# Superblock 1's second product by seven products of halves, sums of w_out made earlier, and 32 writes issued by GpSimd

## The chip, the cores and the metric

The kernel runs on one core of a Trainium2 chip. The metric is the device time of one execution in microseconds. Five engines take part: TensorE (PE, matrix products), VectorE (DVE), ScalarE (ACT), GpSimd (POOL) and SyncE (SP), which in this kernel issues DMA transfers. Each engine works through its own instructions in the order of the program and waits where an instruction needs what another engine or a transfer has not yet delivered.

## The reference

Attention inside chunks of 64 positions, then a feed-forward network on the result, whose rows are x [4608 tokens, 512]:

```python
scores = scale * np.matmul(q_c, k_c.transpose(0, 1, 2, 4, 3))     # q, k, v: [8, 8, 576, 64], chunk = 64
scores = scores - np.max(scores, axis=-1, keepdims=True)
attn = np.exp(scores)
attn = attn / (np.sum(attn, axis=-1, keepdims=True) + 1e-09)
out = np.matmul(attn, v_c)
...
x = np.ascontiguousarray(attn_out.transpose(0, 2, 1, 3)).reshape(B * S, H * D)
...
h = x @ w_in                                                      # [4608, 512] x [512, 2048]
g = np.where(h > 0.0, h, alpha * (np.exp(np.minimum(h, 0.0)) - 1.0))
return (g @ w_out).astype(np.float32)                             # [4608, 2048] x [2048, 512]
```

## The kernel before

**Tiling.** The tokens are taken in nine blocks of TB = 512, the 2048 hidden units in NF = 16 hidden tiles of 128. x @ w_in is called the first product here, g @ w_out the second. Every operand is split in a high and a low float32r part, and a product of two operands is three matmuls of 512 columns: high by high, high by low, low by high (`three`, L434, so nearly all big matmuls have that line). ACT copies the high part (`ghi`), POOL or DVE subtracts it to get the low one (`glo`). In a second product of hidden tile f and token tile tt the order on PE is hi·hi, lo·hi, hi·glo or the like.

**Stages.** Blocks 0 to 2 are plain: 192 + 192 big matmuls each. Blocks 0 and 1 also prepare the weights; block 2, called the third block below, is written out in `THIRD_BLOCK`, `EVEN` and `ODD`. The six other blocks form three superblocks of two. A superblock takes its first product by seven products of halves (Strassen's scheme in Winograd's form, 336 big matmuls for 384); the sums and differences of operand halves that this needs are made ahead and lie in DRAM: those of w_in in `a_dram`, those of w_out in `w_dram`. Superblocks 0 and 1 are written out by hand: eight pairs of hidden tiles (`FIRST_PAIR`, `SECOND_PAIR`, `PAIR`), and then a list of 16 lines, `KEPT`, in which the second product of the superblock's second block runs (`split_kept`, "G": ACT and POOL or DVE split one hidden tile). Their second product is direct: 384 big matmuls each, with w_out's low parts loaded again and again from `lo_dram` by `load_lo`. Superblock 2 is emitted by `Plan`, a list scheduler that holds jobs with a due time, a cost per engine, and the places read and written; its second product goes by seven products of halves too, with B operands from `w_dram` loaded into a ring of places.

**Attention.** One token tile of 128 tokens at a time, an item of the lists for each step. DVE transposes q and k (L351), takes maxima and sums and scales, and transposes the scores (L388); four transfers of 32 KB (`turned<-unturned`) swap parts of them.

**Sums of w_out.** Class `Sums` makes them for one j (two hidden tiles): `whole` a and b (high plus low), `sum` c and d (four subtractions of 128 x 256), `high` e (an ACT copy of 128 x 1024), `low` f (a subtraction of 128 x 1024), then the writes to `w_dram`. Eight of them are needed before superblock 2: j = 2 in superblock 0, 3, 0, 1 and 4 in superblock 1, j = 5, 6, 7 at the start of the plan. The four unsummed quarters of w_out go to `w_dram` as well: high parts by `write_raw` (12 transfers of 256 KB), low parts by `write_raw_low`, all from SP and in the second half of superblock 1.

**What sets the order.** Outside the plan every item is issued where the lists name it, on each engine in that order; SP's transfers also run in that order, and an instruction that waits holds up all behind it on its engine. The last lines set `dynamic_dma_scratch_size=512`.

Of the kernel before, what the change touches and what calls it, by code (L numbers as in the profile page):

```python
# [20 lines left out]
def kernel(  # L21
# [19 lines left out]
    nc = tc.nc  # L41
# [522 lines left out]
    class Sums:  # L564
# [34 lines left out]
        def write(self, which=(0, 1)):  # L599
            for lo in which:  # L600
# [5 lines left out]

    def sum_step(j: int, part: str):
        if part == "a":
            place = kept_st[j][:, :4 * TB] if j < 2 else flat(g_kept[:, {2: 8, 3: 8, 4: 0}[j]:][:, :4])
            early_sums[j] = Sums(j, place, [weights[0][3][:, (2 * j + i) % (NF // 2), :] for i in range(2)])  # L610
        sums = early_sums[j]
        if part in "ab":
            sums.whole("ab".index(part), nc.gpsimd if j in (2, 3) else nc.vector)
        elif part in "cd":
            for t in ((1, 3), (2, 4))["cd".index(part)]:
                sums.sum(t, nc.gpsimd if j in (2, 3) else nc.vector)
        elif part == "e":
            sums.high()
        elif part == "f":
            sums.low()  # L620
            sums.write((0,))
        else:
            sums.write((1,))

    def write_raw(n: int, lo: int):
        half, i = divmod(n, 3)
        row, col = W_PARTS[i + 1]
        for d in range(2):
            nc.sync.dma_start(
                out=w_dram[4 + i, 2 * half + d, :, :, lo, :],  # L630
                in_=weights[half][2 + lo][:, 4 * d + row:4 * d + 4:2, col * HALF:(col + 1) * HALF].bitcast(F32))

# [96 lines left out]
    class Pair:  # L729
# [22 lines left out]
        def product(self, i: int):  # L752
            to = y_ps if i in (2, 5, 3) else x_ps
            (ah, al), (bh, bl) = a_operand(i), b_operand(PRODUCTS[i][1])
            for k in range(2):
                three(to, ah[:, k, :], al[:, k, :], bh[:, k, :], bl[:, k, :],
                      i in (1, 2, 5) and k == 0, k == 1, onto=i not in (1, 2, 5))
            if self.g + 1 < 2 * NG:
                load_a(self.g + 1, i)

        def keep(self, i: int):
# [233 lines left out]
    def warm(n: int):  # L995
# [3 lines left out]
        for i in range(n):  # L999
# [76 lines left out]
    )  # L1076
    VECTOR = (0, 8, 9, 10, 11, 12, 13, 15)
    MORE_PAIR = {(1, "p1"): "a", (1, "p6"): "b", (1, "p7"): "c", (1, "p3"): "d", (2, "p5"): "e", (2, "p3"): "f",
                 (3, "p3"): "g"}
    FIRST_SUMS = {(7, "p2"): "w0a", (7, "p6"): "w0b", (7, "p5"): "w0c", (7, "p7"): "w0d", (7, "p4"): "w1a",  # L1080
                  (7, "p3"): "w1b"}
    MORE_KEPT = ({
        7: "w4a", 8: "w4b", 9: "w4c", 10: "w4d", 11: "w4e", 12: "w4f w4g",
    }, {
        0: "L0", 1: "L1", 2: "L2 w0e", 3: "L3 w0f", 4: "w0g", 5: "w1c", 6: "w1d", 7: "w1e W0",
        8: "w1f w1g W1", 9: "L4 L5 W2", 11: "R0 L6 W3", 12: "R1", 13: "L7 W4", 14: "R2", 15: "R3 W5",
    })
# [132 lines left out]
    for f in range(NF):  # L1220
# [69 lines left out]
    def do(item: str):  # L1290
# [6 lines left out]
        elif item[0] == "L":  # L1297
            write_raw_low(int(item[1]))
        elif item == "P":
            second_products()  # L1300
        elif item == "Q":
            second_next()
        elif item == "S":
            store(*unstored.pop())
        elif item[0] == "x" and len(item) > 1:
            name, cols = item[1:3], slice(TB)
            if item[1] == "B":
                name = item[1:4]
            elif item[3:4] in ("a", "b"):
                cols = slice(T2) if item[3] == "a" else slice(T2, TB)  # L1310
            prepare(name, cols)
        elif item[0] == "A":
            load_a(0, int(item[1]))
        elif item[0] == "R":
            load_entry(2 * ENTRIES + int(item[1]))
# [4 lines left out]
    run = (PLAIN - 1) * TB, o_tiles(), b_half_place  # L1320
    for f in range(NF):
        for item in THIRD_BLOCK.get(f, ODD if f % 2 else EVEN).split():
# [42 lines left out]

    x_ps, y_ps = [ps_h.tile([P, TB], F32, name="h") for _ in range(2)]
    preparing, pair = True, None
    for sb in range(2):
        n0 = (PLAIN + 2 * sb) * TB
        run = n0, o_tiles(), a_half_place  # L1370
        for g in range(NG):
            before, pair = pair, Pair(sb * NG + g)
            for item in ((FIRST_PAIR, SECOND_PAIR)[g] if not sb and g < 2 else PAIR).split():
                if item[0] == "p":
                    pair.product(int(item[1]))
                elif item[0] == "c":
                    pair.keep(int(item[1]))
                elif item[0] == "d":
                    pair.add(int(item[1]))
                elif item in "45":  # L1380
                    if before:
                        next(before.parts["3" if item == "5" else item], None)
                elif item in "123":
                    next(pair.parts[item])
                else:
                    do(item)
                for part in MORE_PAIR.get((g, item), "").split():
                    do(f"w{2 + sb}{part}")
                if sb and (g, item) in FIRST_SUMS:
                    do(FIRST_SUMS[g, item])  # L1390
        halves_kept, o_last = iter(range(NF)), o_tiles()
        run = n0 + TB, o_last, b_half_place
        for f, line in enumerate(KEPT):
            for item in line.split() + MORE_KEPT[sb].get(f, "").split():
                if item == "4":
                    next(pair.parts["4"], None)
                elif item == "G":
                    split_kept(next(halves_kept))
                else:
                    do(item)  # L1400

    LATE_SUMS = 5, 6, 7
    units = {}
    NSPLIT = 7
    STEP = 6 * 227
# [408 lines left out]
                for m, name in enumerate(("t1", "T1", "t3", "t2", "T2", "t4", "T4", "T3", "B22")):  # L1814
                    add_prepare(at + .5 * m, name, cols)

    T0 = 4 * 7 * PAIRS * 2
    leftover, queue[:] = list(queue), []
    for when, (job, f, tt, hi, lo) in zip([T0 - 1 + .05 * i for i in range(4)] + [T0 - .5 + .05 * i for i in range(4)],
                                        leftover):  # L1820
# [9 lines left out]
        if last:  # L1830
# [12 lines left out]
    def add_sums(t: float, j: int, turn: int):  # L1843
        made = {}

        def begin():
            made[0] = Sums(j, kept_st[turn][:, :4 * TB],
                           [weights[0][3][:, (2 * j + i) % (NF // 2), :] for i in range(2)])

        def load():  # L1850
            begin()
# [2 lines left out]
        def whole(engine):  # L1854
# [54 lines left out]
```

## Time and profile before

| | us |
|---|---|
| runs | 836.88, 841.43, 843.36 |
| median | 841.43 |
| profiled execution | 835.11 |
| its span, 15864 instructions | 833.3 |
| stretch 317 to 448: pairs of superblock 0 | 131 |
| stretch 448 to 492: KEPT of superblock 0 | 44 |
| stretch 492 to 672: superblock 1 | 180 |
| stretch 672 to 833: superblock 2 with the tail | 161 |

Durations below come from the one profiled execution, which was faster than the three timed runs. In the profile's rows a name stands for a tile, `out<-in`, a number such as L723 for a line of the kernel; SPq is SP's issue of transfers, and its duration includes what it waits for. The L numbers of before and after differ for one operation: the subtraction of a high part is L723 before and L744 after in the superblocks, L479 in the plain blocks in both.

### The profile page before, as it was taken

The page shows a single profiled execution, that of the slowest core. Times are in us where ns is not written, and L with a number is a line of the kernel's source. Part 1 is how long each engine was busy: PE and PEld are TensorE (multiplying, and loading weights), DVE is VectorE, ACT ScalarE, POOL GpSimd, SP SyncE. Part 2 cuts the span into 40 slices and gives each one's busy share as a digit, 9 for nine tenths or more (in the row PEclk, how much of TensorE's full clock was granted, in tenths as well). Part 3 has the DMA queues.
Part 4 walks back from the last instruction along what each step waited for, and adds up shares of the span by engine and source line. Part 5 has one row for each costly group of instructions (what it writes and reads, how often), then busy time and mean ns, then how long its engine had stood idle before and what let it go on. Part 6 is the DMA issues. An engine that isn't in the chain of part 4 may idle for free.

```text
span 833.3 us, 15864 instructions
## 1 busy us (share of the span) xinstructions
PE 815.4 (98%) x5901; PEld 666.6 (80%) x5901; DVE 587.8 (71%) x859; ACT 497.7 (60%) x853; POOL 152.7 (18%) x133
## 2 busy tenths in 40 slices
PE   7899999999999999999999999999999999999997
PEld 6788888878888888888888888877878887888885
DVE  5999997666775769665666866655667586557974
ACT  5999875444554447666656346655566356776551
POOL 0000014446311211411113213211115020000100
PEclk9999999999999999999999999999999999999999
DMA  9875855856687777698987677789838999665655
GB/s 256 251 219 199 262 168 160 273 184 205 228 227 225 206 200 216 191 262 243 269 261 232 188 198 209 201 238 243 260 98 253 310 324 287 194 187 199 220 187 148
DMA packets 204973, 185.09 MB, mean 222 GB/s; under 512 B 76896, under 2 KB 186976, under 8 KB 204896
## 3 DMA queue, kind: packets, MB, share of 16 engines
q1 hardware_dynamic: 204896, 184.08, 74.7%
q8 instruction: 47, 0.77, 0.4%
q14 instruction: 30, 0.25, 0.1%
HBM read 137.36 MB, written 42.99 MB: 216 GB/s over the span
## 4 chain that ended last, share of the span: by engine, by line
PE 90%; DMA 4%; ACT 2%; SPq 2%; DVE 1%; issue 1%; DVEq 0%; ACTq 0%
PE o L434 46%; PE h L434 38%; PE ps_a L248 2%; PE ps_a L256 2%; SPq L206 1%; DMA turned<-unturned 1%; DMA ring<-a_dram 1%; PE h L451 1%; DMA v_sb<-in_v_dram 1%; DMA st<-in_moe_w_in_dram 1%; DMA ring<-w_dram 1%; PE ps_a L315 1%; PE ps_a L270 0%; ACT e L712 0%; ACT xhi L425 0%
## 5 line engine op out<-in xcount | busy, mean ns | idle before, releaser
L434 PE MATMUL o<-wo_hi,ghi 128*128 128x512 f32 x352 | 138.9, 395 | 0.0
L434 PE MATMUL o<-wo_hi,glo 128*128 128x512 f32 x352 | 137.4, 390 | 0.0
L434 PE MATMUL o<-wo_lo,ghi 128*128 128x512 f32 x352 | 137.2, 390 | 0.0
L434 PE MATMUL h<-xhi,wi_hi 128*128 128x512 f32 x276 | 96.0, 395 | 0.7 <-ACT kept L762 0.7
L434 PE MATMUL h<-xlo,wi_hi 128*128 128x512 f32 x276 | 94.5, 389 | 0.0
L723 POOL TENSOR_TENSOR glo<-e,ghi 128x512 fp32r<-128x512 f32 x32 | 41.7, 1304 | 214.2 <-ACT ghi L721 214.2
L434 PEld LDWEIGHTS o<-wo_hi,glo 128*128 128x128 f32 x352 | 66.1, 188 | 14.6 <-DVE glo L479 0.9
L434 PEld LDWEIGHTS o<-wo_hi,ghi 128*128 128x128 f32 x352 | 66.1, 188 | 14.5 <-ACT ghi L476 0.2
L434 PEld LDWEIGHTS o<-wo_lo,ghi 128*128 128x128 f32 x352 | 66.1, 188 | 13.3
L434 PE MATMUL h<-xhi,wi_lo 128*128 128x512 f32 x180 | 70.2, 390 | 0.0
L434 PEld LDWEIGHTS h<-xhi,wi_hi 128*128 128x128 f32 x276 | 51.7, 188 | 12.2 <-ACT kept L762 1.1
L434 PEld LDWEIGHTS h<-xlo,wi_hi 128*128 128x128 f32 x276 | 51.8, 188 | 10.4
L434 PE MATMUL o<-wo_hi,wo_lo 128*128 128x512 f32 x192 | 59.8, 390 | 0.0
L471 DVE SCALAR_TENSOR_TENSOR e<-e,h 128x512 f32<-128x512 f32 x48 | 32.8, 684 | 25.6 <-ACT e L469 25.4
L434 PE MATMUL h<-wi_lo,wi_hi 128*128 128x512 f32 x192 | 50.7, 399 | 0.0
L510 POOL TENSOR_TENSOR kept<-wi_hi,wi_lo 128x512 f32<-128x512 f32 x16 | 21.3, 1349 | 156.6 <-DMA kept<-in_k_dram 115.6
L393 ACT COPY unturned<-turned 128x512 f32<-128x512 f32 x28 | 17.4, 621 | 52.2 <-DVE turned L388 51.4
L434 PE MATMUL h<-wo_lo,wi_hi 128*128 128x512 f32 x192 | 48.6, 389 | 0.0
L762 ACT COPY kept<-h 128x512 f32<-128x512 f32 x48 | 28.1, 586 | 32.9 <-PE h L434 32.7
L361 DVE TENSOR_REDUCE mx<-ps_a 128x8 f32<-128x512 f32 x28 | 19.3, 689 | 37.5 <-ACT xf L420 36.8
L716 DVE SCALAR_TENSOR_TENSOR g_kept<-e,g_kept 128x512 f32<-128x512 f32 x32 | 22.6, 705 | 32.6 <-ACT e L713 32.6
L468 ACT ACTIVATE e<-h 128x512 f32<-128x512 f32 x48 | 28.8, 599 | 27.3 <-PE h L434 24.9
(203 smaller groups left out, 1793.2 us busy)
## 6 DMA issues: line engine op xcount, KB each, us to landing
wi_hi<-a_dram SPq DMA_DIRECT2D x112, 256.0 KB, 4.9
wo_lo<-lo_dram SPq DMA_DIRECT2D x36, 512.0 KB, 5.8
ring<-a_dram SPq DMA_DIRECT2D x56, 256.0 KB, 3.6
ring<-w_dram SPq DMA_DIRECT2D x28, 512.0 KB, 3.7
kept<-in_q_dram SPq DMA_DIRECT2D x100, 128.0 KB, 3.5
kept<-in_k_dram SPq DMA_DIRECT2D x100, 128.0 KB, 4.0
v_sb<-in_v_dram SPq DMA_DIRECT2D x32, 256.0 KB, 5.7
st<-in_moe_w_in_dram SPq DMA_DIRECT2D x16, 512.0 KB, 4.5
```

Source lines behind the costliest of these rows:

```text
L206: nc.sync.dma_start(out=dst[p0:p0 + n], in_=src[b, :, s0:s0 + n, :].rearrange("h s d -> s h d"))
L248: nc.tensor.matmul(scores[halves[c], j, hp, :], lhsT=qT[halves[j], hp, halves[c]], rhs=kT[halves[j], hp, halves[c]], start=True, stop=True,)
L256: nc.tensor.matmul(x_ps[halves[j], c, hp, :], lhsT=v_sb[halves[c], 2 * hp + j, :], rhs=aT[halves[c], :, j * NK + hp], start=True, stop=True,)
L361: nc.vector.tensor_reduce(out=mx, in_=self.scores, axis=AX.X, op=ALU.max)
L393: nc.scalar.copy(out=unturned, in_=turned)
L434: nc.tensor.matmul(ps, lhsT=a, rhs=b, start=start, stop=stop, skip_group_check=onto)
L468: nc.scalar.activation(out=e, in_=h, func=AF.Relu, scale=-1.0)
L471: nc.vector.scalar_tensor_tensor(out=e, in0=e, scalar=-1.0, in1=h, op0=ALU.add, op1=ALU.max)
L510: nc.gpsimd.tensor_tensor(out=out, in0=a, in1=b, op=op)
L716: nc.vector.scalar_tensor_tensor(out=to, in0=e, scalar=-1.0, in1=c, op0=ALU.add, op1=ALU.max)
L723: engine.tensor_tensor(out=lo, in0=e, in1=hi.bitcast(F32), op=ALU.subtract)
L762: nc.scalar.copy(out=c21 if i == 4 else self.kept[i - 1], in_=x_ps)
```

## The change

Superblock 1 is no longer written out: the hand-written pairs and KEPT run once, for superblock 0, and `superblock(1)` and `tokens(1)` (eight attention tiles) go through the plan ahead of superblock 2. Its second product is by seven products of halves. Since `w_dram` is needed one superblock earlier, the sums of w_out move forward: j = 4, 5 into the third block, j = 0, 3 into the pairs, j = 1 into KEPT, j = 2, 6, 7 into the plan. Up to the plan they run on POOL, but for j = 1 on DVE, and their writes are cut in halves of 256 KB and issued by POOL. The 12 writes of unsummed high parts ("W0" to "W5", two each) are issued by POOL in KEPT; the low parts are written by SP in the second block. `load_lo` runs for 20 pairs of hidden tiles instead of 36 (5·NG, 3·NG), and there are 28 loads of `w_dram` more. In KEPT the splits given to DVE are now those of f = 0, 3, 4, 5, 15; three G items move within their line.

```diff
+        def write_half(self, lo: int, half: int, queue=nc.gpsimd):
+            of = slice(2 * half, 2 * half + 2)
+            queue.dma_start(
+                out=w_dram[of, self.j // 2, :, self.j % 2, lo, :].rearrange("i p w -> p i w"),
+                in_=self.place[:, lo].rearrange("p (i d) -> p i d", i=4)[:, of])
...
         elif part == "f":
-            sums.low()
-            sums.write((0,))
+            sums.low(engine)
         else:
-            sums.write((1,))
+            lo, half = divmod("ghij".index(part), 2)
+            sums.write_half(lo, half)
+
+    def sums_place(j: int):
+        if j == 4:
+            return flat(io)
+        if j == 5:
+            return kept_st[2][:, :4 * TB]
+        return flat(g_kept[:, {0: 8, 3: 12, 1: 0}[j]:][:, :4])
+
+    def spread(line: str, more: str):
+        items, more = line.split(), more.split()
+        for i, item in enumerate(more):
+            items.insert((i + 1) * len(line.split()) // (len(more) + 1) + i, item)
+        return items
...
-            nc.sync.dma_start(
+            (nc.sync if lo else nc.gpsimd).dma_start(
                 out=w_dram[4 + i, 2 * half + d, :, :, lo, :],
...
-            if len(uses) + RING <= 5 * NG:
+            if len(uses) + RING <= 3 * NG:
                 load_lo((f - 1 + 2 * RING) % NF)
...
-        "Q Q xt3 z Q Q h G",
-        "Q Q xT3 q Q Q G",
-        "Q Q xB22 k Q Q l G",
+        "Q Q xt3 z G Q Q h",
+        "Q Q G xT3 q Q Q",
+        "Q Q G xB22 k Q Q l",
...
-    VECTOR = (0, 8, 9, 10, 11, 12, 13, 15)
...
+    VECTOR = (0, 3, 4, 5, 15)
+    SUMS_ON_VECTOR = (1,)
+    RAW_LOW = (2, 4, 6, 8, 10, 12)
+    MORE_THIRD = {
+        2: "w4a", 3: "w4b", 4: "w4c w4d", 5: "w4e w4f", 6: "w4g w5a", 7: "w4h w5b", 8: "w4i w5c w5d", 9: "w4j w5e",
+        10: "w5f", 11: "w5g", 12: "w5h", 13: "w5i", 14: "w5j",
+    }
...
+    MORE_KEPT = {
+        0: "W0", 1: "W1", 2: "w1a w1b", 3: "w1c", 4: "w1d", 5: "w1e w1f", 6: "w1g W2", 7: "w1h", 8: "w1i W3", 9: "w1j",
+        10: "W4", 11: "R0", 12: "W5", 13: "R1", 14: "R2", 15: "R3",
+    }
...
-    for sb in range(2):
-        n0 = (PLAIN + 2 * sb) * TB
-        run = n0, o_tiles(), a_half_place
...
+    n0 = PLAIN * TB
+    run = n0, o_tiles(), a_half_place
+    for g in range(NG):
+        before, pair = pair, Pair(g)
...
-    LATE_SUMS = 5, 6, 7
+    LATE_SUMS = (2, 0), (6, 6), (7, 18)
...
-    T0 = 4 * 7 * PAIRS * 2
+    T0 = 4 * 7 * PAIRS
...
-        plan.add(t + .9, "SP", dma(2, 3200), lambda: made[0].write(), place, [("sums", j)])
...
+        for i in range(4):
+            plan.add(t + .9 + .5 * i, "SP", dma(1, 800), lambda i=i: made[0].write_half(i // 2, i % 2, nc.sync),
+                     place[i // 2 * 2:i // 2 * 2 + 2], [("sums", j)])
...
-    for s in range(2, NS):
+    for s in range(1, NS):
         superblock(s)
         if s + 1 < NS:
             tokens(s)
```

Three places in the order of instructions follow. The first is POOL in KEPT of superblock 0; `wo_lo` and `glo` are the places of a hidden tile's low part there, `e` and `g_kept` the values it is taken from. Before, behind the pairs' thirteen subtractions, POOL had eight subtractions and nothing else:

```order
L723 TENSOR_TENSOR glo<-e,ghi 128x512 x13
L723 TENSOR_TENSOR wo_lo<-g_kept,wo_lo 128x512 x7
L723 TENSOR_TENSOR glo<-g_kept,ghi 128x512
L723 TENSOR_TENSOR glo<-e,ghi 128x512 x2
L574 TENSOR_TENSOR g_kept<-wo_hi,wo_lo 128x512 x2
```

Now, behind the last subtractions of the pairs (first row), up to hidden tile 8:

```order
L744 TENSOR_TENSOR glo<-e,ghi 128x512 x8
L650 DMA w_dram<-wo_hi 256x1x256 x2
L744 TENSOR_TENSOR wo_lo<-g_kept,wo_lo 128x512
L650 DMA w_dram<-wo_hi 256x1x256 x2
L744 TENSOR_TENSOR wo_lo<-g_kept,wo_lo 128x512 x2
L601 DMA w_dram<-g_kept 128x2x256
L650 DMA w_dram<-wo_hi 256x1x256 x2
L744 TENSOR_TENSOR wo_lo<-g_kept,wo_lo 128x512
L601 DMA w_dram<-g_kept 128x2x256
L744 TENSOR_TENSOR wo_lo<-g_kept,wo_lo 128x512
```

Sixteen writes stand between the ten subtractions and ahead of the last two (those of hidden tiles 13 and 14, behind W5), where none stood; the subtractions are those of f = 1, 2, 6, 7, 8 and on, instead of 1 to 7 and 14.

The second place is POOL in the third block. Before:

```order
L510 TENSOR_TENSOR kept<-kept 128x256 x4
L510 TENSOR_TENSOR kept<-wi_hi,wi_lo 128x512 x2
L510 TENSOR_TENSOR kept<-kept 128x256 x4
L479 TENSOR_TENSOR glo<-e,ghi 128x512 x13
L723 TENSOR_TENSOR glo<-e,ghi 128x512
```

Now the thirteen subtractions of the plain second product (L479) have the two sums between them; `io` and `kept` are the places of j = 4 and 5:

```order
L574 TENSOR_TENSOR io<-wo_hi,wo_lo 128x512
L479 TENSOR_TENSOR glo<-e,ghi 128x512
L574 TENSOR_TENSOR io<-wo_hi,wo_lo 128x512
L479 TENSOR_TENSOR glo<-e,ghi 128x512
L589 TENSOR_TENSOR io<-io 128x256 x4
L479 TENSOR_TENSOR glo<-e,ghi 128x512
L595 TENSOR_TENSOR io<-io 128x1024
L479 TENSOR_TENSOR glo<-e,ghi 128x512
L601 DMA w_dram<-io 128x2x256
```

Nearly every subtraction now stands behind an operation of a sum or a write.

The third place is DVE in superblock 1, around the steps of one attention tile. Before, in the hand-written pairs (L766 adds two partial products, L716 is the last step of ELU, L351 to L388 are attention):

```order
L716 SCALAR_TENSOR_TENSOR e<-e,spare 128x512
L351 STREAM_TRANSPOSE qT<-kept 128x4x4x32
L351 STREAM_TRANSPOSE k_turned<-kept 128x4x4x32
L766 TENSOR_TENSOR g_kept<-h,kept 128x512
L716 SCALAR_TENSOR_TENSOR g_kept<-e,g_kept 128x512
L766 TENSOR_TENSOR g_kept<-h,kept 128x512
L716 SCALAR_TENSOR_TENSOR e<-e,spare 128x512
L361 TENSOR_REDUCE mx<-ps_a 128x8
```

Now, from the plan (L1467 and L1470 add partial products, L1491 is ELU's last step, L1752 splits, L1538 is a sum of the softmax):

```order
L1491 SCALAR_TENSOR_TENSOR g_kept<-e,g_kept 128x512
L1467 TENSOR_TENSOR g_kept<-o_5397,kept 128x512
L1752 TENSOR_TENSOR split<-g_kept,split 128x512
L1491 SCALAR_TENSOR_TENSOR g_kept<-e,g_kept 128x512
L1470 TENSOR_TENSOR g_kept<-g_kept 128x512
L351 STREAM_TRANSPOSE qT<-kept 128x4x4x32
L351 STREAM_TRANSPOSE k_turned<-kept 128x4x4x32
L1538 TENSOR_REDUCE ps_a<-ps_a 128x2x4
```

Additions of partial products (L1470) and splits (L1752), which the direct second product did not need on DVE, stand between the attention's steps now.

More of the change, by code (lines that the diff above doesn't have):

```diff
@@ L597, in low, with write @@
                 op=ALU.subtract)
-        def write(self, which=(0, 1)):
-            for lo in which:
+        def write_half(self, lo: int, half: int, queue=nc.gpsimd):
[3 more added lines that the diff above has]
+                in_=self.place[:, lo].rearrange("p (i d) -> p i d", i=4)[:, of])
+        def write(self):
+            for lo in range(2):
                 nc.sync.dma_start(
@@ L608, in sum_step @@
         if part == "a":
-            place = kept_st[j][:, :4 * TB] if j < 2 else flat(g_kept[:, {2: 8, 3: 8, 4: 0}[j]:][:, :4])
-            early_sums[j] = Sums(j, place, [weights[0][3][:, (2 * j + i) % (NF // 2), :] for i in range(2)])
-        sums = early_sums[j]
+            early_sums[j] = Sums(j, sums_place(j), [weights[j // 4 if preparing == "third" else 0][3][
+                :, (2 * j + i) % (NF // 2), :] for i in range(2)])
+        sums, engine = early_sums[j], nc.vector if j in SUMS_ON_VECTOR else nc.gpsimd
         if part in "ab":
-            sums.whole("ab".index(part), nc.gpsimd if j in (2, 3) else nc.vector)
+            sums.whole("ab".index(part), engine)
         elif part in "cd":
             for t in ((1, 3), (2, 4))["cd".index(part)]:
-                sums.sum(t, nc.gpsimd if j in (2, 3) else nc.vector)
+                sums.sum(t, engine)
         elif part == "e":
@@ L757, in product @@
                       i in (1, 2, 5) and k == 0, k == 1, onto=i not in (1, 2, 5))
-            if self.g + 1 < 2 * NG:
+            if self.g + 1 < NG:
                 load_a(self.g + 1, i)
@@ L1250 @@
             write_lo(NF - 2 + f)
+        if f in RAW_LOW:
+            write_raw(RAW_LOW.index(f), 1)
         next(combining, None)
@@ L1314, in do @@
         elif item[0] == "R":
-            load_entry(2 * ENTRIES + int(item[1]))
+            load_entry(ENTRIES + int(item[1]))
         else:
@@ L1319 @@
     ctx.enter_context(tc.manual_schedule(engines={mybir.EngineType.Pool}))
-    run = (PLAIN - 1) * TB, o_tiles(), b_half_place
+    run, preparing = ((PLAIN - 1) * TB, o_tiles(), b_half_place), "third"
     for f in range(NF):
-        for item in THIRD_BLOCK.get(f, ODD if f % 2 else EVEN).split():
+        for item in spread(THIRD_BLOCK.get(f, ODD if f % 2 else EVEN), MORE_THIRD.get(f, "")):
             if item == "H":
@@ L1367 @@
     preparing, pair = True, None
-    for sb in range(2):
-        n0 = (PLAIN + 2 * sb) * TB
-        run = n0, o_tiles(), a_half_place
[L1371 to L1400, printed above, removed]
@@ L1402 @@
-    LATE_SUMS = 5, 6, 7
+    n0 = PLAIN * TB
+    run = n0, o_tiles(), a_half_place
+    for g in range(NG):
+        before, pair = pair, Pair(g)
+        for item in ((FIRST_PAIR, SECOND_PAIR)[g] if g < 2 else PAIR).split():
+            if item[0] == "p":
+                pair.product(int(item[1]))
+            elif item[0] == "c":
+                pair.keep(int(item[1]))
+            elif item[0] == "d":
+                pair.add(int(item[1]))
+            elif item in "45":
+                if before:
+                    next(before.parts["3" if item == "5" else item], None)
+            elif item in "123":
+                next(pair.parts[item])
+            else:
+                do(item)
+            for part in MORE_PAIR.get((g, item), "").split():
+                do(part)
@@ L1403 @@
+    halves_kept, o_last = iter(range(NF)), o_tiles()
+    run = n0 + TB, o_last, b_half_place
+    for f, line in enumerate(KEPT):
+        for item in spread(line, MORE_KEPT.get(f, "")):
+            if item == "4":
+                next(pair.parts["4"], None)
+            elif item == "G":
+                split_kept(next(halves_kept))
+            else:
+                do(item)
+    LATE_SUMS = (2, 0), (6, 6), (7, 18)
     units = {}
@@ L1842, with add_sums @@
                      [("G", 3, tt)], [])
-    def add_sums(t: float, j: int, turn: int):
-        made = {}
+    def add_sums(t: float, j: int):
+        made, early = {}, j < NG // 2
+        g = 2 if early else 4 + j % 2
         def begin():
-            made[0] = Sums(j, kept_st[turn][:, :4 * TB],
-                           [weights[0][3][:, (2 * j + i) % (NF // 2), :] for i in range(2)])
+            to = flat(g_kept[:, 4 * g:4 * g + 4]) if early else g_more_of(g)
+            made[0] = Sums(j, to, [weights[0][3][:, (2 * j + i) % (NF // 2), :] for i in range(2)])
         def load():
@@ L1857, in whole @@
             made[0].whole(0, engine)
-        place = [("stage", turn, b) for b in range(4)]
+        place = [("G", g, b) for b in range(4)]
         raw = [("s", i, l) for i in range(4) for l in range(2)] + [
-            ("G", i, b) for i in ((4, 5) if j < NG // 2 else (6, 7)) for b in range(4)]
+            ("G", i, b) for i in ((4, 5) if early else (6, 7)) for b in range(4)]
         half = {"DVE": (350, 423), "POOL": (700, 740)}
-        if j < NG // 2:
-            plan.add(t, "SP", dma(1, 1500), load, [], place[2:])
+        if early:
+            plan.add(t - .9, "SP", dma(1, 1500), load, [], place[2:])
         plan.add(t + .1, None, EITHER, whole, raw + place[2:], place[:1])
@@ L1872, in add_sums @@
         plan.add(t + .8, None, either(2 * TB), lambda engine: made[0].low(engine), place[:2], place[2:])
-        plan.add(t + .9, "SP", dma(2, 3200), lambda: made[0].write(), place, [("sums", j)])
-    for i, j in enumerate(LATE_SUMS):
-        add_sums(T0 + 2 + 12 * i, j, i % 2)
-    for s in range(2, NS):
+        for i in range(4):
+            plan.add(t + .9 + .5 * i, "SP", dma(1, 800), lambda i=i: made[0].write_half(i // 2, i % 2, nc.sync),
+                     place[i // 2 * 2:i // 2 * 2 + 2], [("sums", j)])
+    for j, t in LATE_SUMS:
+        add_sums(T0 + t, j)
+    first_n = (PLAIN + 4) * NTT
+    later[first_n], later[first_n + 1] = attention.now, attention.following
+    later[first_n + 2] = attention.after
+    for s in range(1, NS):
         superblock(s)
```

12 lines of the change are left out of this document (2 added, 10 removed), and 4 rows, old and new, of the table MORE_PAIR.

## The prediction

> **What bounds the kernel now.** I read the page from the top: the share of each engine, the chain that ended last, and the queue table.
>
> ```profile
> span 833.3 us, 15864 instructions
> PE 815.4 (98%) x5901; PEld 666.6 (80%) x5901; DVE 587.8 (71%) x859; ACT 497.7 (60%) x853; POOL 152.7 (18%) x133
> PE 90%; DMA 4%; ACT 2%; SPq 2%; DVE 1%; issue 1%; DVEq 0%; ACTq 0%
> q1 hardware_dynamic: 204896, 184.08, 74.7%
> ```
>
> TensorE (PE) is busy 98% of the span and carries 90% of the chain, so time goes down only by giving PE less to do or by filling its few gaps. GpSimd (POOL) is busy 18%, and all bulk traffic runs on one hardware queue; no transfer that POOL issues is in this trace. The table of stretches says where the gaps are. The rows are: end of the first block, third block, the pairs of superblock 0, its second-product list (KEPT), all of superblock 1 written out by hand, all of superblock 2 from the planner, and three pieces.
>
> ```profile
> core 0: us, PE busy (x) PEld busy (x) DVE busy (x) ACT busy (x) POOL busy (x), PEclk, DMA share, GB/s
> 30.00:118.00 88.00, 88.00 (x736) 70.72 (x735) 84.46 (x119) 79.98 (x149) 1.09 (x1) 1.00 0.72 226
> 215.00:317.00 102.00, 102.00 (x943) 82.99 (x933) 71.48 (x105) 50.76 (x87) 20.06 (x16) 1.00 0.75 208
> 448.00:492.00 44.00, 44.00 (x253) 36.08 (x252) 34.97 (x44) 19.16 (x30) 11.88 (x8) 1.00 0.75 209
> 492.00:672.00 180.00, 177.06 (x1210) 144.64 (x1209) 111.88 (x159) 100.33 (x167) 42.17 (x32) 1.00 0.78 228
> 672.00:833.00 161.00, 154.90 (x681) 127.32 (x679) 112.29 (x177) 92.65 (x157) 4.36 (x3) 0.99 0.70 216
> 770.00:790.00 20.00, 20.00 (x90) 16.55 (x89) 20.00 (x33) 10.11 (x17) 3.50 (x2) 1.00 0.66 216
> ```
>
> Superblock 1 takes 180 us, of which PE is idle 2.94; superblock 2, with the tail, 161. The clock is granted in full throughout, so PE's time is its number of matmuls.
>
> **Term 1: 48 matmuls go.** Neighbouring rows of PE's timeline in the third block give the pace.
>
> ```profile
> 273.07 0.39 PE L434 MATMUL o<-wo_lo,ghi 128*128 128x512 f32 x1
> 273.30 0.39 PE L434 MATMUL o<-wo_hi,glo 128*128 128x512 f32 x1
> 273.53 0.39 PE L434 MATMUL o<-wo_hi,ghi 128*128 128x512 f32 x1
> ```
>
> One matmul starts every 0.2275 us (the 0.39 is its modelled length, and overlaps the next). The direct second product of a superblock is 2 blocks x 4 token tiles x 16 hidden tiles x 3 = 384 matmuls, that by seven products of halves 7/8 of it, 336. Small matmuls (scores, transposes) are unchanged in number. So 48 x 0.2275 = **-10.9 us**, all on the path since PE is at full pace there.
>
> **Term 2: the waits of the hand-written pairs of superblock 1.** The chain of waits of PE in this stretch, and one instance of it:
>
> ```profile
> PE ps_a L256 <- DMA turned<-unturned: 2.2, 3, 1.2
> PE h L434 <- ACT kept L762: 0.7, 1, 0.7
> 545.88 5.30 SPq L650 DMA_DIRECT2D wi_hi<-a_dram  x3
> 551.27 1.26 SPq L399 DMA_DIRECT2D turned<-unturned  x1
> 556.37 0.97 PE L256 MATMUL ps_a<-turned,v_sb 64*64 64x64 f32 x32 [0.83 <-DMA turned<-unturned]
> ```
>
> The attention's swap of 32 KB stands on SP's queue behind three loads of A operands, which stand for 5.30 us until PE has used their places; PE then waits for the swap. After the change these pairs are the planner's, which loads A operands into a ring and places the swaps by due times. I take the whole 2.2 + 0.7 = **-2.9 us**; if the eight attention tiles wait in the plan as they do here, 0.
>
> **Term 3: third block.** Two sums of w_out (j = 4, 5) are made here now, on POOL with one copy each on ACT, and eight writes leave POOL. Their costs, by the same operations elsewhere, and the slack at the tightest place:
>
> ```profile
> L589 POOL TENSOR_TENSOR g_kept<-g_kept 128x256 f32<-128x256 f32 x8 | 6.4, 823 | 0.2
> L574 POOL TENSOR_TENSOR g_kept<-wo_hi,wo_lo 128x512 f32<-128x512 f32 x4 | 5.6, 1404 | 2.7 <-DMA wo_lo<-lo_dram 2.7
> L592 ACT CAST kept<-kept 128x1024 fp32r<-128x1024 f32 x5 | 5.3, 1053 | 1.9 <-DVE kept L589 1.9
> L723 POOL TENSOR_TENSOR glo<-e,ghi 128x512 fp32r<-128x512 f32 x32 | 41.7, 1304 | 214.2 <-ACT ghi L721 214.2
> 270.85 1.29 POOL L479 TENSOR_TENSOR glo<-e,ghi 128x512 fp32r<-128x512 f32 x1 [5.55 <-ACT ghi L476]
> ```
>
> Per sum POOL does 2 x 1.40 + 4 x 0.82 + one subtraction of 1024 columns, which I take as 2 x 1.30: 8.7 us; two sums 17.4, beside the 20.06 it has in 102 us. There is room on average. But POOL's glo of an odd row ends at 272.14 and PE needs it at 273.30: slack 1.16 us. A sum operation that is just begun when ghi arrives holds it for at most its length: 1.40 is late by 0.24, the 1024-column one (2.6) by 1.4. ACT's 1.05 us copy just fits. The items are spread between a line's steps, so few meet the worst spot: **+0.8 us**; bounds 0, and 8 odd rows x 1.4 = 11. In the pairs the slack is larger:
>
> ```profile
> 374.37 1.30 POOL L723 TENSOR_TENSOR glo<-e,ghi 128x512 fp32r<-128x512 f32 x1 [8.13 <-ACT ghi L721]
> 381.99 0.39 PE L434 MATMUL o<-wo_hi,glo 128*128 128x512 f32 x1
> ```
>
> This glo ends at 375.67, 6.3 us before PE reads it, so sums j = 0 and 3 there are free; they stop being free at some 5 us a write.
>
> **Term 4: KEPT.** Sixteen writes of 256 KB stand here on POOL between the subtractions that PE's second product reads. No such issue is in the trace. The rows nearest to it are the same writes issued by SP, their landing times, and those of other 256 KB writes:
>
> ```profile
> 665.69 1.25 SPq L629 DMA_DIRECT2D w_dram<-wo_hi  x2
> w_dram<-wo_hi SPq DMA_DIRECT2D x12, 256.0 KB, 5.3
> a_dram<-wi_lo SPq DMA_DIRECT2D x8, 256.0 KB, 4.1
> out_dram<-io SPq DMA_DIRECT2D x8, 256.0 KB, 2.9
> 446.25 1.30 POOL L723 TENSOR_TENSOR glo<-e,ghi 128x512 fp32r<-128x512 f32 x1 [5.46 <-ACT ghi L721]
> 451.44 1.29 POOL L723 TENSOR_TENSOR wo_lo<-g_kept,wo_lo 128x512 fp32r<-128x512 f32 x1 [0.68 <-ACT wo_lo L721]
> 488.04 0.39 PE L434 MATMUL o<-wo_hi,glo 128*128 128x512 f32 x1
> L723 DVE TENSOR_TENSOR wo_lo<-g_kept,wo_lo 128x512 fp32r<-128x512 f32 x10 | 6.8, 684 | 2.8 <-ACT wo_lo L721 2.8
> ```
>
> What a write holds POOL for lies between SP's issue, 1.25 / 2 = 0.63 us, and the landing of the same write, 5.3. I take 1.2: SP's figure times the ratio of POOL to DVE for one subtraction, 1304 / 684 = 1.9, an estimate. POOL is free at 446.25 + 1.30 = 447.55. Sixteen writes are 19.2 us; the subtractions up to that of hidden tile 13 are nine, 11.7; together 30.9, done by 478.5, and PE reads that tile's low part at 488.04. The tight place is the start: W0's two writes, one subtraction, W1's two, the next: 447.55 + 2.4 + 1.3 + 2.4 + 1.3 = 454.95, and before the change POOL had done these two by 452.73. The second product takes a hidden tile every 2.7 us (44 / 16), so this is near its due time: **+1 us**; bounds 0 and, at 5.3 a write, the 40 of rival A. DVE gives up the subtractions of five late tiles here and takes sum j = 1 for them: the same to 2 us.
>
> **Term 5: superblock 1 in the plan.** It is superblock 2's work plus eight attention tiles, whose small matmuls stand on PE so:
>
> ```profile
> 505.36 0.69 PE L248 MATMUL ps_a<-k_turned,qT 64*64 64x64 f32 x32
> 505.87 0.65 PE L256 MATMUL ps_a<-turned,v_sb 64*64 64x64 f32 x32
> ```
>
> PE: 672 big matmuls x 0.2275 = 152.9, and eight tiles of some 1.1 (505.36 to 506.52, less the overlap at the end), together 161.5 us. DVE: 235 instructions by my count of the new order. At the 0.606 us each of the row 770:790 that is 142 us, at the 0.634 of row 672:833 (112.29 / 177) 149, at the 0.710 of row 30:118 (84.46 / 119) 167. So DVE goes from 62% to about 92% of its stage, and I expect bursts in which PE waits: **+2 us**, bounds 0 and 167 - 161.5 = 5.5. Rows 30:118 and 770:790 say that DVE at 96 to 100% need not cost PE anything.
>
> **Term 6: transfers.** 28 loads of B from w_dram (512 KB) are added, 16 loads of w_out's low parts (512 KB) go: +6.3 MB, some 28 us at the mean 222 GB/s, spread over stages that have a share of 0.70 to 0.78. SP has one issue more in all, but 32 writes less ahead of its loads in the early stages. I take **+0.7** for a loading burst at the new stage's start; bounds 0 and 3.
>
> **Sum.** -10.9 - 2.9 + 0.8 + 1 + 2 + 0.7 = -9.3. The profiled execution took 835.11 (833.3 of span and 1.8 around it), so 825.8 on its terms. It was faster than all three timed runs (836.88 to 843.36), so against the median of 841.43 I forecast **832**. Its own range is 828 to 837: nothing hidden lost at one end, terms 3 and 5 at half their upper bounds at the other. One per cent is 8.4 us, about what a measurement of this kernel tells from no change.
>
> **Rival A, slower: POOL's writes go one at a time.** If POOL can hand on a write only when the one before has landed, each holds it for its landing L, and the subtractions queue behind. In KEPT the sixteenth write goes out no earlier than 447.55 + 15 L, then the subtraction of 1.3, which PE needs at 488.04: a stall of 15 L - 39.2 us. At L = 2.9 that is 4 (net -5, 836), at 4.1 it is 22 (net +13, **854**), at 5.3 it is 40 (net +31, 872). It cancels the gain at L = 3.2. For it: the same writes land after 5.3 us from SP, in pairs, and KEPT's other traffic has a share of 0.75. Against: on SP issue and landing are well apart (0.63 and 5.3). That the writes were cut to 256 KB each would fit such a limit, but 12 of the 32 had this size already.
>
> The Trainium skill, "DMA: Bandwidth & Descriptors", section "SWDGE vs HWDGE vs iDMA", has GpSimd write each descriptor by software into a ring in SBUF; with its 16 bytes a descriptor, and the 512 bytes that the kernel's last lines leave for this, a write of 256 rows of 1 KB over 16 engines (17 places of 32) would not fit beside another. No trace here shows it. By the same page's fit ("Anatomy of one DMA", 2.0 us + bytes / 436e3) a write takes 2.6 us, and rival A would cost nothing.
>
> The Trainium skill, "SBUF — State Buffer", in its box on the "DVE blocks DMA" trap, says that GpSimd cannot write descriptors while DVE holds their shared port; its pair of figures is 0.62 us alone and 3.1 beside DVE. At 3.1 for L the stall of rival A would be 7 us. KEPT's DVE is busy 34.97 of 44 us, and no row of before tells what it would do to a write.
>
> **Rival B: DVE becomes the bound of superblock 1.** At the price of 0.710 an instruction the stage lasts 167 us instead of 161.5, and the attention's swaps come late as well: of term 2 half is kept. The net is -9.3 - 2 + 5.5 + 1.5 = -4.3, **837**. For: ACT and DVE both fill there; against: the 20 us at 100% without a wait.
>
> **Rival C: the gain is eaten before superblock 1.** Odd rows of the third block wait for POOL at most of their eight places (term 3 at 11 instead of 0.8): net +1, **842**. The order puts a sum operation on POOL ahead of nearly every glo there; but a glo is late only if the operation began less than its length before.
>
> **How the numbers follow.** Forecast 0.44, A 0.33, B 0.15, C 0.08. A's time is spread: a third below L = 3.2, a fifth near the cancelling point, the rest above 3.8. Faster by over 1%: two thirds of the forecast and 0.05 of A, 0.34; slower: half of A and little else, 0.20; within: the rest, 0.46. The range reaches from 827 to A at L = 4.2, 856; beyond lie about 0.13.
>
> **What would show it.** The count of big matmuls falls from 3264 to 3216. A queue for POOL's writes appears with 8.4 MB. If the forecast holds, POOL's timeline in KEPT has a subtraction within 1.5 us of each write, and PE waits there for nothing over 1 us; superblocks 1 and 2 take about 162 us each, DVE over 0.85 of the former. If A holds, POOL shows idle time ahead of the subtractions behind a write, and PE waits for POOL's wo_lo and glo between 448 and 500 with L readable from the issue table; if B, PE waits for DVE in superblock 1; if C, for POOL's glo in the third block. Wrong altogether I would be if the clock fell or a plan waited for the low halves of w_dram, which no row lets me price.

## The result and the profile after

| | before | changed |
|---|---|---|
| median, us | 839.15 (4 runs, 835.77 to 843.36) | 865.36 (4 runs, 863.57 to 867.21) |
| profiled span, us | 833.3 | 861.8 |

The changed kernel is slower: ratio 1.0325, 95% interval 1.0296 to 1.0355. The forecast was 832 with a range up to 856; the time lies above it. The page of the changed kernel, first the lines that answer to those shown of before (busy time, chain, queues):

```profile
span 861.8 us, 16017 instructions
PE 817.5 (95%) x5853; PEld 664.0 (77%) x5853; DVE 616.9 (72%) x915; ACT 524.0 (61%) x990; POOL 182.7 (21%) x172
PE 74%; issue 6%; ACT 5%; DMA 5%; DVE 4%; POOL 3%; SPq 3%; DVEq 0%; ACTq 0%; POOLq 0%
q1 hardware_dynamic: 205552, 182.51, 71.6%
q0 software_dynamic: 2560, 8.39, 2.5%
```

PE has 48 instructions fewer (3216 big matmuls, as the change says) and yet 2.1 us more busy time; its share of the chain fell from 90 to 74%. POOL came in with 3%, and "issue", time in which an engine waited for nothing that the profile names, rose from 1 to 6%. The new queue carries POOL's 8.39 MB. The stretches (same columns as before; 492 to 540 is mostly still KEPT, 540 to 672 most of superblock 1):

```profile
215.00:317.00 102.00, 101.40 (x913) 82.30 (x905) 71.69 (x104) 51.73 (x87) 43.56 (x39) 1.00 0.79 227
317.00:448.00 131.00, 127.15 (x923) 102.77 (x916) 87.30 (x129) 80.20 (x137) 40.06 (x36) 0.97 0.78 229
448.00:492.00 44.00, 35.79 (x263) 28.49 (x263) 30.96 (x43) 20.63 (x34) 12.70 (x14) 0.92 0.64 193
492.00:540.00 48.00, 33.70 (x126) 26.47 (x125) 13.79 (x17) 8.29 (x12) 16.51 (x18) 0.83 0.52 163
540.00:672.00 132.00, 128.54 (x966) 103.08 (x965) 109.87 (x177) 105.38 (x261) 15.77 (x12) 1.00 0.87 258
```

PE's waits from 448 to 535 (us in total, times, longest):

```profile
PE o L434 <- POOL wo_lo L744: 21.2, 4, 6.7
PE o L434 <- POOL glo L744: 1.3, 1, 1.3
```

PE loses time from 317 on and above all between 448 and 540, where it waits 22.5 us for low parts that POOL makes; there the granted clock is 0.92 and 0.83. POOL's own timeline in the same place (start, duration, in brackets the idle time ahead and what ended it):

```profile
495.67 1.30 POOL L744 TENSOR_TENSOR wo_lo<-g_kept,wo_lo 128x512 fp32r<-128x512 f32 x1
500.92 0.69 POOL L650 DMA_DIRECT2D w_dram<-wo_hi  x1 [3.95 <-issue]
505.87 0.69 POOL L650 DMA_DIRECT2D w_dram<-wo_hi  x1 [4.25 <-issue]
506.47 1.37 POOL L744 TENSOR_TENSOR wo_lo<-g_kept,wo_lo 128x512 fp32r<-128x512 f32 x1
511.21 0.74 POOL L601 DMA_DIRECT2D w_dram<-g_kept  x1 [3.37 <-issue]
514.29 0.69 POOL L650 DMA_DIRECT2D w_dram<-wo_hi  x1 [2.34 <-issue]
517.02 0.69 POOL L650 DMA_DIRECT2D w_dram<-wo_hi  x1 [2.04 <-issue]
517.61 1.40 POOL L744 TENSOR_TENSOR wo_lo<-g_kept,wo_lo 128x512 fp32r<-128x512 f32 x1
...
525.55 0.69 POOL L650 DMA_DIRECT2D w_dram<-wo_hi  x1 [4.67 <-issue]
```

An issue itself takes 0.7 us; 2 to 5 us of idle time stand ahead of each of these, with the subtraction behind them. In the trace's packets no write of the 32 is issued sooner than 0.64 us after the last packet of the write before has ended. Counted from landings it is sharper: each of the 19 issues that POOL had to wait for starts 0.30 to 0.31 us after the write before has landed. That is the picture of rival A.

To compare stages of kernels that are shifted against each other, I take them between the same matmuls of PE: hidden tile 8 of the third block (start), its last tile, hidden tile 14 of the pairs' second product, hidden tile 14 of KEPT's, the end of the span.

| us | third block | pairs | KEPT | all behind |
|---|---|---|---|---|
| before | 42.2 | 123.5 | 46.4 | 341.2 |
| changed | 43.5 | 131.1 | 75.9 | 331.3 |
| difference | +1.3 | +7.6 | +29.5 | -9.9 |

The sum is +28.5, the difference of the spans. So superblock 1 in the plan brought 9.9 us, and the pairs and KEPT of superblock 0 lost 37. Ahead of the first place the two profiles differ by 0.1; among all the profiles below that place lies between 279.9 and 283.4 us, so spans of single executions differ by up to 3.5 us from the start-up alone, and the stages or the medians are what to compare.

### The profile page after: what moved, and what is told of

The parts are those of the page before. It is cut to its first block, busy times and chain, and to the rows that moved or that the text cites. A ratio compares the mean times of both kernels' runs of the same rounds, so it can differ in the third digit from the quotient of the medians.

```text
span 861.8 us, 16017 instructions
## 1 busy us (share of the span) xinstructions
PE 817.5 (95%) x5853; PEld 664.0 (77%) x5853; DVE 616.9 (72%) x915; ACT 524.0 (61%) x990; POOL 182.7 (21%) x172
## 3 DMA queue, kind: packets, MB, share of 16 engines
q0 software_dynamic: 2560, 8.39, 2.5%
## 4 chain that ended last, share of the span: by engine, by line
PE 74%; issue 6%; ACT 5%; DMA 5%; DVE 4%; POOL 3%; SPq 3%; DVEq 0%; ACTq 0%; POOLq 0%
PE o L434 37%; PE h L434 32%; DMA ring<-a_dram 2%; PE ps_a L248 2%; PE ps_a L256 1%; SPq L227 1%; POOL wo_lo L744 1%; PE h L451 1%; DMA turned<-unturned 1%; POOL w_dram L650 1%; DMA kept<-in_k_dram 1%; ACT ps_a L1562 1%; SPq L206 1%; POOL glo L744 1%; SPq L399 1%
## 5 line engine op out<-in xcount | busy, mean ns | idle before, releaser
L434 PE MATMUL o<-wo_hi,ghi 128*128 128x512 f32 x272 | 108.0, 397 | 0.0
L434 PE MATMUL o<-wo_hi,glo 128*128 128x512 f32 x272 | 106.5, 392 | 1.3 <-POOL glo L744 1.3
L434 PE MATMUL o<-wo_lo,ghi 128*128 128x512 f32 x272 | 106.4, 391 | 0.0
L434 PEld LDWEIGHTS o<-wo_lo,ghi 128*128 128x128 f32 x272 | 51.2, 188 | 10.3
L434 PE MATMUL o<-wo_hi,wo_lo 128*128 128x512 f32 x96 | 35.8, 456 | 21.2 <-POOL wo_lo L744 21.2
L434 PE MATMUL o<-split,ring 128*128 128x512 f32 x216 | 51.1, 390 | 0.0
L434 PEld LDWEIGHTS o<-split,ring 128*128 128x128 f32 x216 | 40.5, 188 | 8.4
L434 PEld LDWEIGHTS o<-wo_hi,wo_lo 128*128 128x128 f32 x96 | 21.2, 226 | 27.6 <-POOL wo_lo L744 22.9
L476 ACT CAST ghi<-e 128x512 fp32r<-128x512 f32 x48 | 29.8, 620 | 18.3 <-DVE e L471 18.2
L434 PE MATMUL h<-split,ring 128*128 128x512 f32 x168 | 40.5, 393 | 0.2 <-DMA ring<-w_dram 0.2
L1488 ACT ACTIVATE e<-e 128x512 f32<-128x512 f32 x64 | 39.6, 631 | 1.0
```

Source lines behind the costliest of these rows:

```text
L434: nc.tensor.matmul(ps, lhsT=a, rhs=b, start=start, stop=stop, skip_group_check=onto)
L476: nc.scalar.copy(out=ghi, in_=e)
L1488: nc.scalar.activation(out=units[u], in_=units[u], func=AF.Exp, scale=-1.0)
```

## The experiments

A descriptor is an entry that tells a DMA engine what to move; for a transfer that POOL issues, the entries go into the memory that `dynamic_dma_scratch_size` sets aside. Theory: this memory holds one such write, so each issue waits for the write before, and the subtractions queue behind. Rivals: POOL takes one write at a time by nature; VectorE keeps POOL from issuing; the loss is in POOL's added sums, or in the splits' new places, and not in the writes.

### More memory for GpSimd's descriptors: 1024 bytes

```diff
-                     dynamic_dma_scratch_size=512)
+                     dynamic_dma_scratch_size=1024)
```

> The changed kernel with 1024 instead of 512 bytes for GpSimd's descriptors; not one instruction differs. Theory 'full ring': a write of 256 rows needs 17 places of 16 bytes and 512 bytes hold only one such write, so GpSimd's next write waits for the last packet of the one before. Then with 1024 bytes three writes fit, GpSimd's issues no longer stand at 0.64 us or more after the end of the packets before, the +37 us of the pairs and of KEPT go almost all, and the median is 828 to 836. Rival 'one at a time by nature': GpSimd's queue takes one write at a time whatever its memory; the time stays at 865 and so does the pattern of issues. Rival 'shared port': GpSimd is held while VectorE works; the time stays within 3 us of 865 too, but issues then need not follow the packets' ends.

Measured: 835.85 us (before 839.88, measured beside it; ratio 0.995, 0.9925 to 0.9976). Without a change of one instruction 29.5 us went. POOL's timeline in KEPT:

```profile
481.11 1.44 POOL L650 DMA_DIRECT2D w_dram<-wo_hi  x2
482.33 1.83 POOL L744 TENSOR_TENSOR wo_lo<-g_kept,wo_lo 128x512 fp32r<-128x512 f32 x1
484.11 0.74 POOL L601 DMA_DIRECT2D w_dram<-g_kept  x1
488.26 0.68 POOL L650 DMA_DIRECT2D w_dram<-wo_hi  x1 [3.42 <-issue]
489.27 0.69 POOL L650 DMA_DIRECT2D w_dram<-wo_hi  x1 [0.33 <-issue]
```

and what is left of PE's waits there:

```profile
PE o L434 <- POOL wo_lo L744: 4.0, 1, 4.0
```

Three writes now leave within 3.7 us, and the fourth, at 488.26, comes 0.31 us after the first of them (481.11) has landed. The same holds for all five issues of this trace that POOL waited for: each follows, by 0.31 to 0.32 us, the landing of the write three places ahead of it. So the limit is the memory: one write in 512 bytes, three in 1024. "By nature" falls, and so does the shared port, since issues follow landings and not VectorE. The Trainium skill, "DMA: Bandwidth & Descriptors", section "Terms", has descriptors of 16 bytes, which for transfers that GpSimd issues are written to rings in SBUF. By that size, an estimate, a write of 256 rows on 16 DMA engines takes 17 places (16 rows and one that reports the end), of 32 in 512 bytes and of 64 in 1024: the one and the three writes of these traces.

### 2048 bytes

The same edit with 2048.

> The changed kernel with 2048 bytes for GpSimd's descriptors, so seven writes in flight instead of one (512) or three (1024). With 1024 one wait of PE for GpSimd is left in KEPT, 4.0 us with 1.7 us of slow matmuls behind it, at a place where GpSimd issued a fourth write. Theory 'full ring': it goes, KEPT is 44 to 46 us as before the change, and the median is 4 to 6 us below that of 1024 bytes (835.9): 830 to 832. Rival 'the last wait is of the writes' bandwidth or of sources': it stays, 834 to 837.

Measured: **829.88 us** (before 839.03; ratio 0.9911, 0.9882 to 0.994), below both kernels. KEPT's stretch, and behind it POOL's timeline there:

```profile
448.00:492.00 44.00, 44.00 (x312) 36.17 (x311) 36.50 (x43) 21.24 (x36) 25.66 (x27) 1.00 0.85 260
```

```profile
480.68 1.43 POOL L650 DMA_DIRECT2D w_dram<-wo_hi  x2
481.89 1.55 POOL L744 TENSOR_TENSOR wo_lo<-g_kept,wo_lo 128x512 fp32r<-128x512 f32 x1
483.13 0.95 POOL L601 DMA_DIRECT2D w_dram<-g_kept  x1
483.87 1.65 POOL L650 DMA_DIRECT2D w_dram<-wo_hi  x2
485.04 1.81 POOL L744 TENSOR_TENSOR wo_lo<-g_kept,wo_lo 128x512 fp32r<-128x512 f32 x1
```

PE has no gap in this stretch, and none of the 32 issues has idle time ahead. KEPT took 75.9 us with 512 bytes, 50.7 with 1024, 44.9 with 2048. The landing is no faster for it: POOL's writes of raw parts land 6.6 us after issue (median) where it was 3.0; no wait of PE in this trace is for them.

### Writes half as long, 512 bytes

```diff
-            of = slice(2 * half, 2 * half + 2)
-            queue.dma_start(
...
+            for of in (2 * half, 2 * half + 1):
+                queue.dma_start(
...
```

These are 128 rows each; the raw writes are cut in two in the same way.

> The changed kernel with each of GpSimd's 32 writes cut in two of 128 rows (128 KB), so 64 writes, and 512 bytes as before. Full ring: a write needs 9 places, so three fit in 32 places; GpSimd pays 64 x 0.7 us of issue, but waits much less: 832 to 848. One at a time by nature: 64 waits of 2.5 to 4 us each instead of 32 of 3 to 5, so as slow as 865 or slower, up to 890. Shared port: the number of descriptors is about the same (9 for 17, twice), so within 5 us of 865.

Measured: 854.8 us (ratio 1.0181, 1.014 to 1.0222), above the 832 to 848 that I gave this theory, but below 865. POOL's writes do overlap: each of the 18 issues that POOL waited for follows, by 0.31 to 0.32 us, the landing of the write three places ahead of it, so three shorter writes fit. But there are 64 of them, and trains of up to six fill the places again:

```profile
488.18 0.56 POOL L656 DMA_DIRECT2D w_dram<-wo_hi  x1 [0.55 <-issue]
491.82 0.54 POOL L656 DMA_DIRECT2D w_dram<-wo_hi  x1 [3.09 <-issue]
492.67 0.54 POOL L656 DMA_DIRECT2D w_dram<-wo_hi  x1 [0.31 <-issue]
494.12 0.55 POOL L656 DMA_DIRECT2D w_dram<-wo_hi  x1 [0.92 <-issue]
```

KEPT is 64.4 us. The bytes in flight are 3 x 128 KB instead of 256, a gain of half, not the threefold that I had reckoned with.

### All 32 writes from SP

```diff
-        def write_half(self, lo: int, half: int, queue=nc.gpsimd):
+        def write_half(self, lo: int, half: int, queue=nc.sync):
...
-            (nc.sync if lo else nc.gpsimd).dma_start(
+            nc.sync.dma_start(
```

> The changed kernel with all 32 writes issued by SP at the same places of the lists, GpSimd issuing none. Full ring, and any theory that puts the loss on GpSimd's issuing: the stalls of GpSimd go, and the gain of the planned superblock 1 is seen: 828 to 838, unless SP's queue is held by writes that wait for sums. The rival that the loss comes from the sums and splits that GpSimd does, and not from its writes: 855 or more.

Measured: 833.61 us (ratio 0.9938, 0.9909 to 0.9967). The profile is of the slowest of its seven executions, 840.03. KEPT is 44.9 us in it, so GpSimd's larger work is not the loss. Waits for the attention's swap appear instead, in its list of PE's waits, and with them the third block takes 46.7 us and the pairs 128.2:

```profile
PE ps_a L256 <- DMA turned<-unturned: 4.0, 2, 2.4
```

The swaps stand on SP's queue too, some of them now behind writes that wait for sums; that these writes hold them up is likely and was not tried apart. POOL as issuer is thus no mistake; its memory was.

### Only the raw writes from SP

The second half of the diff above alone.

> The changed kernel with only the 12 writes of unsummed high parts issued by SP; the 20 half writes of sums stay on GpSimd. By the list, KEPT then has 4 writes on GpSimd instead of 16. Full ring and one at a time alike: the +29 us of KEPT go to within 3 us, the +8 of the pairs and +1 of the third block stay: 836 to 843. If the loss in KEPT came from DVE's or GpSimd's larger share of splits instead: 860.

Measured: 840.06 us (ratio 0.9997, 0.9974 to 1.002). KEPT falls to 46.1 us, the pairs stay at 130.4. So KEPT's 29.5 us are the twelve raw writes among sixteen, as expected. The pairs' 7 us need only the eight half writes there. One wait of PE, 3.4 us in the changed kernel and 3.2 here, is the largest part, and with the slow matmuls behind it (2.8 us in the changed kernel, counted from 371.91 to 382.89 against the same matmuls of before) it is most of them. It is not for glo but for VectorE. Of the changed kernel, VectorE, then POOL, then PE:

```profile
371.58 3.62 DVE L737 SCALAR_TENSOR_TENSOR g_kept<-e,g_kept 128x512 f32<-128x512 f32 x1 [0.25 <-ACT e L734]
...
370.10 0.73 POOL L601 DMA_DIRECT2D w_dram<-g_kept  x1 [3.55 <-issue]
370.85 2.56 POOL L574 TENSOR_TENSOR g_kept<-wo_hi,wo_lo 128x512 f32<-128x512 f32 x2
373.36 1.26 POOL L744 TENSOR_TENSOR glo<-e,ghi 128x512 fp32r<-128x512 f32 x1
374.58 3.37 POOL L589 TENSOR_TENSOR g_kept<-g_kept 128x256 f32<-128x256 f32 x4
...
376.87 2.93 PE L434 MATMUL h<-wo_lo,wi_hi 128*128 128x512 f32 x6 [3.41 <-DVE spare L787]
```

The write waits 3.55 us; POOL's work behind it is dammed up and then runs without a gap, and the VectorE operation beside it lasts 3.62 us instead of 0.69.

### The same, with the sum j = 3 on VectorE

```diff
-    SUMS_ON_VECTOR = (1,)
+    SUMS_ON_VECTOR = (1, 3)
```

> The variant whose 12 raw writes are SP's (512 bytes, 840.06), with the sum j = 3 of the pairs made on VectorE instead of GpSimd; its writes stay GpSimd's. In that variant PE pauses 3.6 us at 376 in the pairs, behind one VectorE operation (L737) of 3.41 us that lasts 0.69 elsewhere and that stands beside two sum operations, a subtraction and another sum operation of GpSimd without a gap. Theory 'VectorE is held by GpSimd's train of operations': with the train shortened the operation is back under 1.5 us, the pause goes, and the pairs are 4 to 6 us shorter (834 to 837). Rival 'it is the write's wait alone that makes things late': the pause stays, 839 to 842.

Measured: 835.42 us (ratio 0.9971, 0.9948 to 0.9993). The variant without this edit had 840.06 and a ratio of 0.9997 (0.9974 to 1.002), beside other runs of before. The ratios differ by 2.2 us and their intervals overlap, so the gain in time is likely and not shown. The same VectorE operation:

```profile
376.06 0.68 DVE L737 SCALAR_TENSOR_TENSOR g_kept<-e,g_kept 128x512 f32<-128x512 f32 x1
```

It is short again, and POOL is idle beside it, so POOL's train had held it. But the pairs took 128.2 us, only 2.2 less, where I had expected 4 to 6: three waits of 0.6 to 1.3 us stand where one of 0.7 and one of 3.2 were. So the hold is seen, and its share of the pairs' loss is about a third, by one profile each. The rest I put down to the writes' waits, which was not tried apart; with 2048 bytes, and all sums on GpSimd, the pairs take 125.0.

### Half the traffic of w_dram in superblock 1

```diff
+        planned_first = e < 2 * ENTRIES
...
+        elif planned_first:
+            o, d = divmod(e, PAIRS)
+            nc.sync.dma_start(out=slot[:, :1].bitcast(F32), in_=w_dram[W_OPS.index(SECOND[o]), d][:, :1])
```

> The same with 2048 bytes, and in the planned superblock 1 each load of w_dram takes 256 KB instead of 512 KB; the other half of the place keeps what it held (this leaves out half of the B operands, so the product is not the reference's). 28 loads shorter, -7.3 MB. Theory that transfers bound the new stage's middle (waits of PE for the ring of operands, 3.5 us in all with 1024 bytes, share of the DMA engines 0.81 over 168 us): these waits and their slow matmuls go, 4 to 6 us less than ring2048. Rival that ScalarE and VectorE, or the order of SP's queue, set those waits: less than 1.5 us of difference.

With 2048 bytes as well. Each load of w_dram in superblock 1 leaves out half of its bytes, so half of the B operands there are stale and the product is not the reference's; the matmuls are the same in number.

Measured: 829.09 us (ratio 0.9894, 0.9863 to 0.9926) against 829.88 with 2048 bytes alone. The stretch of the new stage, with 2048 bytes and then with less traffic:

```profile
492.00:660.00 168.00, 165.12 (x1154) 132.23 (x1153) 139.89 (x225) 128.06 (x304) 18.75 (x14) 1.00 0.83 254
```

```profile
492.00:660.00 168.00, 165.03 (x1153) 132.22 (x1152) 140.10 (x225) 127.78 (x304) 18.73 (x14) 1.00 0.71 211
```

The DMA share fell from 0.83 to 0.71, and PE's idle time stayed at 2.9 to 3.0 us. So the amount of traffic does not bound this stage, and my theory falls.

## Why the prediction was wrong, point by point

**Term 4, KEPT, is the step that failed**, at "I take 1.2": the hold of a write on POOL was set by its issue alone, from SP's 0.63 scaled. The issue is in fact 0.69 to 0.83 us in KEPT, less than that; but ahead of the next one POOL waits until the write before has landed, 2.4 to 5.7 us after its own issue (mean of the sixteen 3.6), and 0.31 us more. Both ends were in the text; I chose the near one because on SP issue and landing are well apart, and put 0.33 on the other. The 512 bytes in the kernel's last lines, quoted beside the rival, decided it. The Trainium skill, "DMA: Bandwidth & Descriptors", "Anatomy of one DMA", has the fit from which the prediction took 2.6 us a write. In the changed kernel's trace, writes that met next to no other packet landed 2.4 to 2.8 us after issue, near it, and those beside other traffic with a DMA share over 0.75 took 3.7 to 7.1.

The rival's formula, 15 L - 39.2, has the right path but not the right L. L was to be the landing, and with the mean of 3.6 it gives some 15 us. From the first issue of KEPT, at 456.31, to the sixteenth, at 525.55, pass 69.2 us instead of 15 L: 54.6 of landings, 4.6 between landings and the issues that follow them, and 10 between the fourth landing and the fifth issue, most of it this wait of POOL for ACT:

```profile
479.57 1.29 POOL L744 TENSOR_TENSOR wo_lo<-g_kept,wo_lo 128x512 fp32r<-128x512 f32 x1 [9.80 <-ACT wo_lo L742]
```

69.2 - 39.2 is 30.0, and KEPT lost 29.5. That L = 4.1, the value behind the rival's 854, gives about the 22.5 us that PE waited is chance: the formula counts the whole delay of that matmul, and PE's waits are only a part of it. One count of the prediction is off by one: POOL has eleven subtractions in KEPT, ten of them up to that of hidden tile 13, 13.0 us and not 11.7, which changes nothing.

**What rival A lacked, 854 against 865, are two things.** First, the pairs: "free ... until some 5 us a write" counted PE's need of glo alone, and one write at a time. Three half writes stand in a row there, a late glo also keeps its place `e` from the next ELU (ACT waits 2.6 us for one), and, dammed up, POOL holds VectorE: +7.6 instead of 0. Second, KEPT lost 29.5 instead of 22 and 1, by the idle stretch above and the steps of 0.31. On PE's side the 29.5 are 22.5 us of waits and slow matmuls behind them. PE's timeline of the changed kernel around one wait:

```profile
486.32 0.62 PE L434 MATMUL o<-wo_hi,wo_lo 128*128 128x512 f32 x2
486.77 0.39 PE L434 MATMUL o<-wo_lo 128*128 128x512 f32 x1
491.17 0.99 PE L434 MATMUL o<-wo_hi,wo_lo 128*128 128x512 f32 x2 [4.01 <-POOL wo_lo L744]
491.95 0.63 PE L434 MATMUL o<-wo_lo 128*128 128x512 f32 x1
492.38 1.06 PE L434 MATMUL o<-wo_hi,wo_lo 128*128 128x512 f32 x2
493.23 0.63 PE L434 MATMUL o<-wo_lo 128*128 128x512 f32 x1
493.66 1.06 PE L434 MATMUL o<-wo_hi,wo_lo 128*128 128x512 f32 x2
494.51 0.57 PE L434 MATMUL o<-wo_lo 128*128 128x512 f32 x1
494.92 0.62 PE L434 MATMUL o<-wo_hi,wo_lo 128*128 128x512 f32 x2
```

Three matmuls take 0.68 us before the wait, 1.28 behind it (492.38 to 493.66), and are back at full rate from 494.9. The granted clock is 0.57 from 491.0 to 494.5. Behind the five waits of KEPT this adds 7.7 us by the same count: 22.5 + 7.7 is the 29.5 measured, to within 0.7. This says where PE's time went; since the last subtraction sets KEPT's end, PE at full rate would in part have waited longer instead, which was not tried.

**The other terms held as a sum.** Third block +0.8 forecast, +1.3 measured; rival C is excluded. The 48 matmuls of term 1 went (3264 to 3216). Terms 1, 2, 5 and 6 together were -10.9 - 2.9 + 2 + 0.7 = -11.1 for all behind KEPT; measured -9.9, and -10.3 with 2048 bytes; 5 and 6 were not measured singly. Rival B is excluded as well: VectorE is busy 139.89 of 168 us (0.83, below the forecast's 0.92) in that stage with 2048 bytes, and PE waits 0.7 us for it. Term 2's old waits went, and shorter ones for operands (1.3 us for the ring) came. With the wait of term 4 taken away by memory alone, the whole sum is seen: stages +1.0, +1.5, -1.5, -10.3, together -9.3, and medians 829.88 against 839.03, -9.2. That this is the forecast's sum to the tenth is luck: the pairs came out 1.5 above their term and KEPT 2.5 below, and the ratio 0.9911 gives -7.5 us, with an interval of -5 to -10.

## What to carry to other kernels

Before giving transfers to GpSimd, count the descriptors of one (rows over engines, and one more) against the memory set aside for them: an issue that finds it full stops everything behind it on that engine, and transfers of which just one fits run strictly one behind the other. Price a wait of TensorE with the slow matmuls behind it: with 1024 bytes, one wait of 4.0 us left KEPT 5.8 us longer than with 2048. And where two bounds of an unknown cost lie far apart and a number in the code decides between them, work that number out before choosing the near one.

## What the runs showed of the hardware

In the changed kernel an issue of GpSimd that finds its descriptor memory full starts 0.30 to 0.31 us after the landing that makes room. In KEPT there, a pause of PE of 4 to 7 us is followed by 7 to 12 matmuls at up to 0.43 us instead of 0.2275, 1.6 to 2.3 us more each time; after pauses near 1 us it was mostly under 0.5. The Trainium skill, "TensorE: Matmul & The Clock Gate", part 1, has half the clock after an idle window of some 3.4 us. The half agrees, but here shorter pauses did it too: with writes half as long, a pause of 2.38 us at 464.30 was followed by 3.4 us at a granted clock of 0.50. A VectorE operation of 0.69 us lasted 3.62 beside a train of GpSimd operations and 0.68 without it.
